# Attention's small column operations (negated maxima, edge sums, the added constant) moved from VectorE to ScalarE

## Chip, core and metric

The kernel runs on one core of a Trainium2 chip. Its time is the device time of one execution in microseconds (us). The engines are TensorE (PE in the profile; PEld is its weight load), VectorE (DVE), ScalarE (ACT), GpSimd (POOL) and SyncE (SP, which issues transfers). Each runs its own list of instructions in order, and they wait for each other by semaphores.

## What is computed

Block-sparse attention over 4 batches, 8 heads, 768 tokens and 64 columns a head, and behind it a mixture of 4 experts on the 3072 tokens with 512 columns.

```python
scores = scale * np.matmul(q, k.transpose(0, 1, 3, 2))
mask = np.abs(blk_i - blk_j) <= window          # blocks of 32, window 1
mask = mask | (blk_i == 0) | (blk_j == 0) | (blk_i == n_blocks - 1) | (blk_j == n_blocks - 1)
# ... and 3 sampled key blocks for each query block
scores = np.where(mask, scores, -1000000000.0)
scores = scores - np.max(scores, axis=-1, keepdims=True)
attn = np.exp(scores)
attn = attn / (np.sum(attn, axis=-1, keepdims=True) + 1e-09)
out = np.matmul(attn, v)
# then, on x = out by token:
p = domain_probs / (domain_probs.sum(-1, keepdims=True) + 1e-09)
for e in range(E):
    h = np.maximum(x @ w1[e], 0.0)
    y += p[:, e:e + 1] * (h @ w2[e])
```

## The kernel before

The batches run one behind the other, with attention one batch ahead: batch 0's attention alone (the first 77 us), then, while the experts work on batch b, the attention of batch b+1. Behind batch 3's attention only expert work is left. The order on all five engines is the order in which the program is written, so a queue never passes a waiting instruction.

The attention of a batch is 16 units. Four are of the class `Edge`: the first and the last query block, each against all keys in two halves (m = 0 and 1). Twelve are of the class `Group`: up to four query blocks against eight gathered key blocks each, half of the heads at a time. A unit has four steps, S, T, A and X. S makes the scores on TensorE, the maxima on VectorE and the exponentials with their sums on ScalarE. T transposes the probabilities. A multiplies them by the values and divides by the sums, X transposes the result into the experts' input `xr`. In batches 1 to 3 a unit's turn writes X of the unit before last, T of the last one, some expert work, S of the new unit, and then A of the last one. So on VectorE and ScalarE the A of a unit stands right behind the S of the next.

In a Group's S VectorE makes a masked, negated maximum (L372, the tile `mx`) for each of four heads, and ScalarE takes the exponential with this maximum as its bias and leaves the sum in `sums` (L374). A Group's A adds 1e-9 to the four sums (L402), takes the reciprocal (L403) and multiplies the result `o` in PSUM by it into `xg` (L404). An Edge's S makes two maxima (L444), for m = 1 the maximum over both halves (L446), the negated and scaled maximum `nm` (L447), for m = 1 the difference `w` of the maxima (L449), the exponentials (L451) and the exponential of the difference (L454). Its A for m = 1 adds the two halves' sums, the first weighted by `w` (L481, L482), takes the reciprocal (L483), adds the two halves of the result (L486) and multiplies (L489).

Of the experts' work these lines are spoken of. L754 is the first product and L991 (batches 1 to 3) or L827 (batch 0) the second one on TensorE. Their results go to PSUM tiles `w`, `v`, `u` and `po`, and VectorE takes them from there: L801 to L813 and L773 in batch 0, L892, L896, L899, L902 and L869 in the others, L842 adds `po` to the accumulator, L1001 adds to the totals. The tile `w` has one buffer, so the next product into it waits until VectorE has read the last (L902, L813). L914 and L915 (ScalarE, GpSimd) split the hidden layer into two parts for the second product. L158 copies sampled key blocks, L643, L679 and L718 split weights, L385 and L463 copy transposed probabilities from PSUM.

Of the kernel before, what the change touches and what calls it, by code (L numbers as in the profile page):

```python
# [8 lines left out]
F32 = mybir.dt.float32  # L9
# [3 lines left out]
AF = mybir.ActivationFunctionType  # L13
ALU = mybir.AluOpType
# [3 lines left out]
P = 128  # L18
# [5 lines left out]
def attention_moe_kernel(ctx: ExitStack, tc, qb, kb, vr, sampled, sampled_t, probs, w1, w2, out):  # L24


    nc = tc.nc
# [12 lines left out]
    SCALE = 1.0 / 8.0  # L40
# [7 lines left out]
    const = ctx.enter_context(tc.tile_pool(name="const", bufs=1))  # L48
# [6 lines left out]
    at = ctx.enter_context(tc.tile_pool(name="at", bufs=2))  # L55
# [171 lines left out]

    one = const.tile([1, 1], F32, name="one")
    nc.vector.memset(one, 1.0)
    warm = const.tile([1, 1], F32, name="warm")  # L230
    nc.scalar.activation(warm, one, AF.Exp)
    zero = p1.tile([P, HS], F32, name="zero")
# [100 lines left out]
    class Group:  # L333
# [53 lines left out]
        def A(self):  # L387
            b, t, u, n = self.b, self.t, self.u, self.n
            vs = gathered[b, t][2]
            o = pool["o"].tile([P, 2 * HH, D], F32, name="o", tag=pool["tag"])  # L390
            for m in range(2 * HH):
                e = slice((2 * HH * u + m) * D, (2 * HH * u + m + 1) * D)
                for k in range(2):
                    for c in range(n // BLOCK):
                        cs = slice(c * BLOCK, (c + 1) * BLOCK)
                        nc.tensor.matmul(o[cs, m], self.pt[:, 2 * m + k, cs], vs[c][:, k, e],  # L396
                                         start=k == 0, stop=k == 1)
            if u == 0:
                xg[0] = at.tile([P, DM], F32, name="xg", bufs=pool["xg"])
            self.xg = xg[0]  # L400
            rec = at.tile([P, 2 * HH], F32, name="rec")
            nc.vector.tensor_scalar(rec[:n], self.sums[:n], 1e-9, None, op0=ALU.add)  # L402
            nc.vector.reciprocal(rec[:n], rec[:n])  # L403
            nc.vector.tensor_mul(self.xg[:n, 2 * HH * D * u:2 * HH * D * (u + 1)]  # L404
                                 .rearrange("p (h d) -> p h d", d=D), o[:n],
                                 rec[:n].unsqueeze(2).broadcast_to([n, 2 * HH, D]))
            if u:
                gathered.pop((b, t))
# [10 lines left out]
    class Edge:  # L419
# [5 lines left out]
        def S(self):  # L425
            m = self.m
            k, q, _ = keys[self.b]
            s = [pool["s"].tile([P, HS], F32, name="sw", tag="s") for _ in range(2)]
            for hp in range(HP):
                e = slice(hp * BLOCK, (hp + 1) * BLOCK)  # L430
                for h in range(2):
                    half = slice(D * h, D * (h + 1))
                    nc.tensor.matmul(s[h][e].rearrange("p (a b) -> p a b", b=BLOCK),  # L433
                                     q[half, self.i, e], k[half, m * NB // 2:(m + 1) * NB // 2, e],
                                     start=True, stop=True)
            if m == 0:
                edge["S"] = [at.tile([P, 2, 2], F32, name=f"edge{j}") for j in range(2)]
                edge["w"] = at.tile([P, 2], F32, name="ew")
            self.mx, self.sums = edge["S"]
            self.w = edge["w"]  # L440
            self.p = pool["p"].tile([P, S], F32, name="pw", tag="p")
            nm = at.tile([P, 2], F32, name="nm2")
            for h in range(2):
                nc.vector.reduce_max(self.mx[:, m, h:h + 1], s[h], axis=AX.X)  # L444
            if m == 1:
                nc.vector.tensor_max(self.mx[:, 1], self.mx[:, 0], self.mx[:, 1])  # L446
            nc.vector.tensor_scalar(nm, self.mx[:, m], -SCALE, None, op0=ALU.mult)  # L447
            if m == 1:
                nc.vector.tensor_sub(self.w, self.mx[:, 0], self.mx[:, 1])  # L449
            for h in range(2):  # L450
                nc.scalar.activation(self.p[:, h * HS:(h + 1) * HS], s[h], AF.Exp, bias=nm[:, h:h + 1],  # L451
                                     scale=SCALE, accum_out=self.sums[:, m, h:h + 1])
            if m == 1:
                nc.scalar.activation(self.w, self.w, AF.Exp, scale=SCALE)  # L454
# [10 lines left out]
        def A(self):  # L465
            vs = keys[self.b][2]
            n = KT // 2
            o = pool["o"].tile([P, 2, D], F32, name="ow", tag=pool["tag"])
            for h in range(2):
                for k in range(n):  # L470
                    for hp in range(HP):
                        cs = slice(hp * BLOCK, (hp + 1) * BLOCK)
                        e = slice((2 * hp + h) * D, (2 * hp + h + 1) * D)
                        nc.tensor.matmul(o[cs, h], self.pt[:, h * n + k, cs], vs[self.m * n + k][:, e],
                                         start=k == 0, stop=k == n - 1)
            if self.m == 0:
                edge["o"] = at.tile([P, 2, D], F32, name="eo", bufs=1)
                pool["copy"](edge["o"], o)
                return
            rec = at.tile([P, 2], F32, name="rec2")  # L480
            nc.vector.tensor_mul(rec, self.sums[:, 0], self.w)  # L481
            nc.vector.scalar_tensor_tensor(rec, rec, 1e-9, self.sums[:, 1], op0=ALU.add, op1=ALU.add)  # L482
            nc.vector.reciprocal(rec, rec)  # L483
            eo = edge["o"]
            for h in range(2):
                nc.vector.scalar_tensor_tensor(eo[:, h], eo[:, h], self.w[:, h:h + 1], o[:, h],  # L486
                                               op0=ALU.mult, op1=ALU.add)
            self.xg = at.tile([P, P], F32, name="xe", bufs=1)
            nc.vector.tensor_mul(self.xg.rearrange("p (h d) -> p h d", d=D), eo,  # L489
                                 rec.unsqueeze(2).broadcast_to([P, 2, D]))  # L490
# [482 lines left out]
    def second7(b, c, i):  # L973
# [20 lines left out]
        for g, dh in (TO_END if last else TO)[n]:  # L994
            if c == 0 and d == 0 and n in FRESH:
                tot[g, dh] = later["a"].tile([P, 2, HS], F32, name="tot", bufs=4)
            t = tot[g, dh][:, d]
            if c == 0 and n in FRESH:
                nc.scalar.copy(t, ps)
            else:  # L1000
                nc.vector.tensor_add(t, ps, t)  # L1001
            if c == NCH - 1 and (LAST_END if last else LAST)[g, dh] == n and d:
                nc.sync.dma_start(bass.AP(out.tensor, out.offset + b * S * DM + dh * (DM // 2) * S + g * HS,
                                          [[S, P], [P * S, 2], [1, HS]]), tot.pop((g, dh)))
# [333 lines left out]
```

## Time and profile before

| | |
|---|---|
| median of 3 runs | 1234.24 us (1231.65 to 1234.75) |
| the profiled execution's time | 1232.82 us |
| its span | 1231.1 us |
| granted clock of TensorE, mean | 0.993 |
| VectorE busy, 413 to 700 us (batch 2's attention within) | 200.10 of 287 us |
| ScalarE busy in the same stretch | 119.25 of 287 us |
| TensorE busy in the same stretch | 281.08 of 287 us |

A row of the profile names line, engine, operation and tiles (out<-in). In a group's row the numbers behind the bar are the busy us, the mean ns of one, and the idle us of the engine before it with what ended it. In the order of time a row gives start and duration in us, the shape and, in brackets, the idle time before it and what released it. A row of waits gives who waited for whom: us in total, times, longest. A wait is named by its last releaser.

### The profile page before, as it was taken

How to read it: one execution, taken by the hardware profiler on the slowest of the kernel's cores; microseconds unless marked ns; L12 is line 12 of the kernel's file. 1: busy time of each engine (PE TensorE's matmuls, PEld its weight loads, DVE VectorE, ACT ScalarE, POOL GpSimd, SP SyncE). 2: the span in 40 equal slices, each digit the busy share in tenths (PEclk: the TensorE clock that was granted, in tenths of full speed). 3: DMA queues.
4: the chain of work that ended last, by engine and by line, in shares of the span. 5: the costliest groups of instructions: out<-in, count | busy, mean ns of one | idle time of the engine just before them, and what ended most of it. 6: DMA issues, size and time to landing. Idle time of an engine off the chain costs nothing.

```text
span 1231.1 us, 32030 instructions
## 1 busy us (share of the span) xinstructions
PE 1189.1 (97%) x12243; PEld 1095.4 (89%) x12243; DVE 808.7 (66%) x1701; ACT 519.8 (42%) x1259; POOL 838.4 (68%) x824
## 2 busy tenths in 40 slices
PE   7899999999999899999999999999999999999997
PEld 4678888888888898989989999989999999999997
DVE  4774757565654667767666867766566676666667
ACT  3864555656552243444533244444533333222221
POOL 7837978888776575767647775766755776666662
PEclk8999999999999899999999999999999999999999
DMA  9986869899979787888969786989876688887874
GB/s 289 264 281 232 312 246 351 290 316 318 307 266 351 227 242 233 259 278 274 270 211 345 227 267 222 286 252 283 285 253 209 219 271 266 258 262 251 255 239 154
DMA packets 214564, 326.81 MB, mean 265 GB/s; under 512 B 17483, under 2 KB 117420, under 8 KB 214412
## 3 DMA queue, kind: packets, MB, share of 16 engines
q1 hardware_dynamic: 207888, 303.53, 76.2%
q0 software_dynamic: 6480, 21.24, 5.8%
q8 instruction: 97, 1.59, 0.6%
q14 instruction: 55, 0.45, 0.1%
q10 hardware_dynamic: 44, 0.00, 0.0%
HBM read 257.02 MB, written 67.68 MB: 264 GB/s over the span
## 4 chain that ended last, share of the span: by engine, by line
PE 79%; DVE 5%; DMA 1%; issue 1%; ACT 1%; SPq 0%; POOL 0%; DVEq 0%; ACTq 0%
PE w L754 19%; PE u L991 15%; PE v L754 14%; PE v L991 12%; PE po L827 8%; PE o L396 3%; PE tp L383 2%; PE s L362 2%; PE s L355 1%; DVE ha L869 1%; PE x L415 1%; DMA pb<-prt 1%; DMA v<-in_vr_dram 1%; PE sw L433 1%; DVE tot L1001 1%
## 5 line engine op out<-in xcount | busy, mean ns | idle before, releaser
L915 POOL TENSOR_TENSOR ho<-ha,ho 128x768 fp32r<-128x768 f32 x165 | 318.3, 1938 | 244.8 <-ACT ho L914 242.0
L754 PE MATMUL w<-xo,wo 128*128 128x384 f32 x1524 | 310.9, 340 | 10.9 <-DVE ha L869 3.5
L754 PEld LDWEIGHTS w<-xo,wo 128*128 128x128 f32 x1524 | 268.8, 189 | 19.5 <-DVE ha L902 3.9
L914 ACT CAST ho<-ha 128x768 fp32r<-128x768 f32 x168 | 139.2, 837 | 269.9 <-DVE ha L869 106.1
L754 PE MATMUL v<-xo,wo 128*128 128x384 f32 x1176 | 238.9, 339 | 1.5 <-DVE xr L417 1.0
L991 PE MATMUL u<-ho,w2o 128*128 128x384 f32 x1128 | 228.2, 338 | 2.3 <-issue 2.3
L754 PEld LDWEIGHTS v<-xo,wo 128*128 128x128 f32 x1176 | 207.7, 189 | 6.4 <-DVE xr L417 1.1
L991 PEld LDWEIGHTS u<-ho,w2o 128*128 128x128 f32 x1128 | 197.0, 188 | 4.6 <-issue 2.9
L991 PE MATMUL v<-ho,w2o 128*128 128x384 f32 x888 | 179.8, 339 | 3.2 <-issue 1.5
L991 PEld LDWEIGHTS v<-ho,w2o 128*128 128x128 f32 x888 | 154.7, 188 | 7.1 <-DVE ha L869 2.7
L1001 DVE TENSOR_TENSOR tot<-v,tot 128x384 f32<-128x384 f32 x184 | 97.9, 552 | 91.6 <-PE v L991 90.3
L1001 DVE TENSOR_TENSOR tot<-u,tot 128x384 f32<-128x384 f32 x180 | 98.8, 552 | 47.9 <-PE u L991 47.8
L827 PE MATMUL po<-w2o,hh 128*128 128x512 f32 x384 | 123.5, 403 | 1.9 <-DVE oacc L842 1.9
L374 ACT ACTIVATE p<-p,mx 128x256 f32<-128x256 f32 (+1 forms) x192 | 95.3, 498 | 50.8 <-DVE mx L372 50.6
L213 POOL DMA_INDIRECT v<-in_vr_dram,vidx x81 | 79.9, 986 | 24.4 <-issue 17.8
L644 POOL TENSOR_TENSOR wo<-r,wo 128x256 fp32r<-128x256 f32 x92 | 72.4, 793 | 32.3 <-ACT wo L643 28.5
L372 DVE CUSTOM_DVE_ANT_1 p<-s,mask 128x256 f32<-128x256 f32 (+1 forms) x192 | 69.8, 419 | 22.0 <-PE s L362 17.0
L869 DVE SCALAR_TENSOR_TENSOR ha<-ha,pb 128x384 f32<-128x384 f32 x84 | 82.5, 982 | 0.0
L827 PEld LDWEIGHTS po<-w2o,hh 128*128 128x128 f32 x384 | 69.0, 188 | 12.6 <-DVE oacc L842 2.7
L827 PE MATMUL po<-w2o,hl 128*128 128x512 f32 x192 | 75.8, 395 | 0.0
L396 PEld LDWEIGHTS o<-v,pt 128*32 128x32 f32 x2816 | 46.1, 110 | 18.5 <-issue 13.5
L396 PE MATMUL o<-v,pt 128*32 128x64 f32 x2816 | 54.6, 221 | 5.1 <-issue 3.1
(169 smaller groups left out, 1627.3 us busy)
## 6 DMA issues: line engine op xcount, KB each, us to landing
w2o<-kept SPq DMA_DIRECT2D x168, 512.0 KB
wo<-kept SPq DMA_DIRECT2D x318, 256.0 KB
kept<-wo SPq DMA_DIRECT2D x106, 256.0 KB
v<-in_vr_dram SPq DMA_DIRECT2D x88, 192.0 KB
kept<-w2o SPq DMA_DIRECT2D x32, 512.0 KB
r<-in_w_dram SPq DMA_DIRECT2D x16, 512.0 KB
r<-in_w_dram SPq DMA_DIRECT2D x32, 256.0 KB
kept<-t SPq DMA_DIRECT2D x32, 256.0 KB
```

The lines of the kernel that those rows point to most:

```text
L213: nc.gpsimd.indirect_dma_start(out=v[:, i, 1 - i], out_offset=None, in_=vr, element_offset=b * S * DM, in_offset=bass.IndirectOffsetOnAxis ...
L372: nc.vector.tensor_tensor_reduce(p.rearrange("p (a b) -> p a b", b=BLOCK), s[h][:n, i], mk, -SCALE, 3.0e38, ALU.add, ALU.min, mx[:n])
L374: nc.scalar.activation(p, p, AF.Exp, bias=mx[:n], scale=-1.0, accum_out=self.sums[:n, m:m + 1])
L396: nc.tensor.matmul(o[cs, m], self.pt[:, 2 * m + k, cs], vs[c][:, k, e], start=k == 0, stop=k == 1)
L644: nc.gpsimd.tensor_sub(o[:, 1], src, f32(o[:, 0]))
L754: nc.tensor.matmul(ps, w[:, wi, t], x[:, xi, t], start=fresh and m == 0, stop=m == 3 * KH - 1, skip_group_check=not fresh)
L827: nc.tensor.matmul(p, a[:, js], w[:, i], start=f == 0 and n == 0, stop=f == FT - 1 and n == 2)
L869: nc.vector.scalar_tensor_tensor(block(g, half), src, 0.0, q, op0=ALU.max, op1=ALU.mult)
L914: nc.scalar.copy(o[:, 0], src)
L915: eng.tensor_sub(o[:, 1], src, f32(o[:, 0]))
L991: nc.tensor.matmul(ps, w[:, j, wi, ds], h[:, hi, j], start=fresh and m == 0, stop=m == 5, skip_group_check=not fresh)
L1001: nc.vector.tensor_add(t, ps, t)
```

## The change

Four small operations move. In a Group's A of batches 1 to 3 (not of batch 0) the constant 1e-9 is added by ScalarE, as a function with a bias by row from a new constant tile `eps`. In an Edge's S the negated, scaled maximum is made by ScalarE, in all batches. In an Edge's A the sum of the second half plus the constant goes to a new tile `last2` on ScalarE, and for each of the two heads the first half's sum, scaled by `w`, is added to it there with scale and bias by row; VectorE's two operations of before are gone. The reciprocals and all that follows stay on VectorE. Lines of the changed kernel below are numbered 2 to 8 higher.

```diff
+    eps = const.tile([P, 1], F32, name="eps")
+    nc.vector.memset(eps, 1e-9)
 ...
             rec = at.tile([P, 2 * HH], F32, name="rec")
-            nc.vector.tensor_scalar(rec[:n], self.sums[:n], 1e-9, None, op0=ALU.add)
+            if b:
+                nc.scalar.activation(rec[:n], self.sums[:n], AF.Identity, bias=eps[:n])
+            else:
+                nc.vector.tensor_scalar(rec[:n], self.sums[:n], 1e-9, None, op0=ALU.add)
             nc.vector.reciprocal(rec[:n], rec[:n])
 ...
-            nc.vector.tensor_scalar(nm, self.mx[:, m], -SCALE, None, op0=ALU.mult)
+            nc.scalar.mul(nm, self.mx[:, m], -SCALE)
 ...
             rec = at.tile([P, 2], F32, name="rec2")
-            nc.vector.tensor_mul(rec, self.sums[:, 0], self.w)
-            nc.vector.scalar_tensor_tensor(rec, rec, 1e-9, self.sums[:, 1], op0=ALU.add, op1=ALU.add)
+            last = at.tile([P, 2], F32, name="last2")
+            nc.scalar.activation(last, self.sums[:, 1], AF.Identity, bias=eps)
+            for h in range(2):
+                nc.scalar.activation(rec[:, h:h + 1], self.sums[:, 0, h:h + 1], AF.Identity,
+                                     bias=last[:, h:h + 1], scale=self.w[:, h:h + 1])
             nc.vector.reciprocal(rec, rec)
```

TensorE's, GpSimd's and SyncE's lists stay as they are. VectorE's list at the fourth Group unit of batch 2, before:

```order
L372 ISA p,mx<-s,mask 128x256
L372 ISA mx 128x1
L402 TENSOR_SCALAR rec<-sums 128x4
L403 RECIPROCAL rec<-rec 128x4
L404 TENSOR_TENSOR xg<-o,rec 128x256
L902 TENSOR_TENSOR ha<-w,ha 128x384
```

and now, with ScalarE's list at the same place behind it (L376 is the exponential, L910 the old L902):

```order
L374 ISA p,mx<-s,mask 128x256
L374 ISA mx 128x1
L408 RECIPROCAL rec<-rec 128x4
L409 TENSOR_TENSOR xg<-o,rec 128x256
L910 TENSOR_TENSOR ha<-w,ha 128x384
```

```order
L376 ACTIVATE p,sums<-p,mx 128x256 x4
L405 ACTIVATE rec<-sums,eps 128x4
L158 ISA
L158 COPY kr_3365<-k 128x128
L898 COPY ha<-v 128x384
```

The add has left VectorE, where it stood behind the last maximum, and stands on ScalarE behind the four exponentials of the next unit and ahead of the key copies; the reciprocal waits for it.

VectorE's list at the first Edge's A in batch 1, before:

```order
L444 TENSOR_REDUCE edge_2894<-sw 128x1 x2
L447 TENSOR_SCALAR nm_2898<-edge_2894 128x2
L481 TENSOR_TENSOR rec_2929<-edge_2518,ew 128x2
L482 SCALAR_TENSOR_TENSOR rec_2929<-rec_2929,edge_2518 128x2
L483 RECIPROCAL rec_2929<-rec_2929 128x2
L486 SCALAR_TENSOR_TENSOR eo<-eo,ew,ow 128x64 x2
L489 TENSOR_TENSOR xe<-eo,rec_2929 128x128
L813 TENSOR_TENSOR z_2824<-w,z_2824 128x384
```

and ScalarE's list at this place now (L456 is the pair of exponentials, L687 and L726 the old L679 and L718, L780 the expert's activation L772):

```order
L726 CAST t_2887<-r_2350 128x512
L452 ACTIVATE nm_2904<-edge_2900 128x2
L456 ACTIVATE pw,edge_2901<-sw,nm_2904 128x384 x2
L487 ACTIVATE last_2936<-edge_2524,eps 128x2
L489 ACTIVATE rec_2935<-edge_2524,last_2936,ew 128x1 x2
L687 CAST w2o<-r_2507 128x512
L780 ACTIVATE hh_2966<-z_2830 128x384
```

The negation stands ahead of the exponentials that use it, and the three new sums behind them; VectorE's list goes from the two maxima straight to the reciprocal.

## Prediction

> **What bounds the kernel now.** I read the page first, for the engine that sets the end: row 1 and the chain that ended last. Then the waits of TensorE, to see what still holds it up.
>
> ```profile
> PE 1189.1 (97%) x12243; PEld 1095.4 (89%) x12243; DVE 808.7 (66%) x1701; ACT 519.8 (42%) x1259; POOL 838.4 (68%) x824
> PE 79%; DVE 5%; DMA 1%; issue 1%; ACT 1%; SPq 0%; POOL 0%; DVEq 0%; ACTq 0%
> ...
> PE w L754 <- DVE ha L869: 3.5, 2, 3.2
> PE w L754 <- DVE ha L902: 3.2, 2, 1.6
> ...
> PE w L754 <- DVE z L813: 1.5, 2, 1.3
> ```
>
> TensorE is busy 97% of a span of 1231.1 us, so some 42 us of idle time are all that any change of the other engines can take away or add to. VectorE (66%) and ScalarE (42%) have room on average; moving work between them is worth only what it does to the moments at which TensorE waits for them. The waits on VectorE are few and short. So the question is not how much VectorE work goes, but whether VectorE reaches the operations that free TensorE's PSUM banks earlier or later.
>
> **What the removed operations cost.** Next the groups by line (busy us, mean ns) and, for two lines, their spread (min/median/max ns).
>
> ```profile
> L402 DVE TENSOR_SCALAR rec<-sums 128x4 f32<-128x4 f32 (+1 forms) x48 | 21.5, 448 | 0.0
> L447 DVE TENSOR_SCALAR nm<-edge 128x2 f32<-128x2 f32 x16 | 7.9, 497 | 0.7
> L482 DVE SCALAR_TENSOR_TENSOR rec<-rec,edge 128x2 f32<-128x2 f32 x8 | 5.2, 644 | 0.3
> L481 DVE TENSOR_TENSOR rec<-edge,ew 128x2 f32<-128x2 f32 x8 | 3.8, 476 | 0.0
> L374 ACT ACTIVATE p<-p,mx 128x256 f32<-128x256 f32 (+1 forms) x192 | 95.3, 498 | 50.8 <-DVE mx L372 50.6
> L643 ACT CAST wo<-r 128x256 fp32r<-128x256 f32 x92 | 36.8, 402 | 45.5 <-DVE r L639 13.1 <-issue 11.8 <-DVE r L637 7.5
> L454 ACT ACTIVATE ew<-ew 128x2 f32<-128x2 f32 x8 | 1.6, 198 | 0.0
> ...
> L402 DVE TENSOR_SCALAR rec<-sums x48: 152/220/1773, 36.3 to 937.0; 128x4 f32<-128x4 f32 x40, 64x4 f32<-64x4 f32 x8
> L403 DVE RECIPROCAL rec<-rec x48: 169/178/181, 36.5 to 937.1; 128x4 f32<-128x4 f32 x40, 64x4 f32<-64x4 f32 x8
> ```
>
> An add on four columns takes 152 ns when nothing is in its way, and up to 1773 ns; the reciprocal behind it never takes more than 181 ns. The stretched ones wait for something other than their own work, and GpSimd (68% busy) is the neighbour that could hold it. From VectorE go 36 of 48 such adds (36 x 448 ns = 16.1 us), 16 negations (7.9 us) and 16 operations of the edge sums (9.0 us): 33 us, of which about 11 are work (68 x 160 ns) and 22 waiting.
>
> ScalarE gets 36 + 16 + 8 + 16 = 76 operations. No such operation is in this trace, so its price is bounded: below by L454, a function on two columns without an operand by row (198 ns); above by that plus what a bias by row adds, read from two groups of 256 columns, 498 ns with one (L374) and 402 without (L643), so 96 ns: 294 ns, and 390 with bias and scale both by row. I take 198 for the negation, 294 for the sum plus constant, 390 for the edge's scaled sum. In all 16 x 198 + 44 x 294 + 16 x 390 ns = 22 us on an engine with 700 us free. That is no cost; the place in its queue is.
>
> The Trainium skill, "ScalarE: Activation LUTs", section Rules for kernel authors, says to give add and mul to VectorE. By unblocked rows (152 against 294 ns) the trace agrees; by the means (448 against 294 ns) it does not, and taken as a rule on busy time alone it would say some 11 us more work on an idle engine: nothing in the sum.
>
> **The place in the queue.** The add of a Group reads sums that were ready long before. On VectorE it stood behind the four masked maxima (L372) of the next unit; on ScalarE it stands behind the four exponentials that consume them, and VectorE's reciprocal now waits for it. This is the fourth unit of batch 2, with both engines and TensorE:
>
> ```profile
> 544.69 0.08 DVE L372 DVE_READ_ACCUMULATOR2_ANT mx<- 128x1 f32 x1
> 544.69 0.90 DVE L402 TENSOR_SCALAR rec<-sums 128x4 f32<-128x4 f32 x1
> 545.62 0.18 DVE L403 RECIPROCAL rec<-rec 128x4 f32<-128x4 f32 x1
> 546.24 0.55 DVE L902 TENSOR_TENSOR ha<-w,ha 128x384 f32<-128x384 f32 x1
> ...
> 545.33 0.49 ACT L374 ACTIVATE p<-p,mx 128x256 f32<-128x256 f32 x1
> 545.73 0.19 ACT L374 ACTIVATION_READ_ACCUMULATOR p<-p,mx 128x1 f32 x1
> 545.83 0.28 ACT L158 COPY kr<-k 128x128 f32 x1
> ...
> 546.85 1.31 PE L754 MATMUL w<-xo,wo 128*128 128x384 f32 x6 [1.61 <-DVE ha L902]
> ```
>
> VectorE is through with its maxima at 544.77, ScalarE with its exponentials at 545.92: 1.14 later, since an exponential takes 0.49 and a maximum 0.34. The new operation can start where L158 starts now (545.83) and ends 0.29 later; with some 0.1 for the signal the reciprocal starts at 546.22, where it started at 545.62. So a wait of about 1.45 takes the place of an add of 0.90, here 0.60 later; where the add was not stretched (0.16), about 1.33 later. Here L902 follows at once and TensorE already waits for it (1.61), so TensorE goes 0.60 later too. That the add is gone from VectorE buys nothing, because its own time lay inside the wait.
>
> Of the 36 units 33 stand behind exponentials. In each I took the lag at the reciprocal (from -0.34 to 1.45, mean 0.94 over the 36), subtracted VectorE's idle gaps in the order in which they follow, and compared what is left with the time between the end of each VectorE operation and the matmul that waits for it. In 25 of the 33 it is eaten by a gap or by TensorE's distance. In eight it reaches TensorE. The first and the last of them:
>
> ```profile
> 227.35 0.18 DVE L403 RECIPROCAL rec<-rec 128x4 f32<-128x4 f32 x1
> 227.98 1.40 DVE L842 SCALAR_TENSOR_TENSOR oacc<-po,pr,oacc 128x512 f32<-128x512 f32 x2
> 228.10 0.19 ACT L374 ACTIVATION_READ_ACCUMULATOR p<-p,mx 128x1 f32 x1
> 229.33 0.63 PE L827 MATMUL po<-w2o,hh 128*128 128x512 f32 x2
> ...
> 898.14 0.18 DVE L403 RECIPROCAL rec<-rec 128x4 f32<-128x4 f32 x1
> 899.86 0.56 DVE L902 TENSOR_TENSOR ha<-w,ha 128x384 f32<-128x384 f32 x1 [0.48 <-PE w L754]
> 898.98 0.18 ACT L374 ACTIVATION_READ_ACCUMULATOR p<-p,mx 128x1 f32 x1
> 900.70 1.03 PE L754 MATMUL w<-xo,wo 128*128 128x384 f32 x5
> ```
>
> First: lag 228.29 + 0.30 - 227.35 = 1.24; the first of the two L842 ends near 228.70, 0.6 before the matmul: 0.69 left. Last: lag 1.32, less the gap of 0.48, less 0.28 of distance and plus 0.06 for the signal: 0.62. The eight add 0.69 + 0.60 + 1.00 + 0.86 + 0.58 + 0.49 + 0.65 + 0.62 = 5.5 us. With the lower price (198 ns) it is 4.7, with 100 ns more 6.4. It is TensorE's time, and TensorE is the bound, so it stays in the total.
>
> **The edge units.** Here the negation goes first on ScalarE, then two exponentials, then the two dependent sums, and VectorE's reciprocal (L483) behind all of it.
>
> ```profile
> 154.91 0.17 DVE L483 RECIPROCAL rec<-rec 128x2 f32<-128x2 f32 x1
> 156.17 0.55 DVE L813 TENSOR_TENSOR z<-w,z 128x384 f32<-128x384 f32 x1
> 153.40 0.61 ACT L718 CAST t<-r 128x512 fp32r<-128x512 f32 x1
> 155.34 0.20 ACT L451 ACTIVATION_READ_ACCUMULATOR pw<-sw,nm 128x1 f32 x1
> 156.77 1.31 PE L754 MATMUL w<-xo,wo 128*128 128x384 f32 x6 [1.33 <-DVE z L813]
> ...
> 469.37 0.17 DVE L483 RECIPROCAL rec<-rec 128x2 f32<-128x2 f32 x1
> 471.52 0.27 PE L495 MATMUL xt<-ident,xe 128*128 128x128 f32 x1
> ```
>
> At 154 ScalarE is free at 154.01, and the negation there ends about when VectorE's did, so the exponentials end at 155.5 as before. Then 0.29 and twice 0.39, overlapping by 0.09 but with a signal between the first two, give 156.35 for the reciprocal instead of 154.91: 1.4 later, L813 follows without a gap, TensorE waits 1.4 longer. At 469 the reciprocal is 1.9 later, but the transpose waits with 1.25 in hand: 0.65. The other four of batches 1 to 3 are no later at the reciprocal than now (their sums are the stretched ones behind the means of 476 and 644 ns), or are caught by a gap. Edge sum 2.1. The negations by themselves change no path: the same length, one signal to another. The mean of 497 ns holds some 0.3 of stretching each; where TensorE waits at the end of such a chain that is spared, perhaps twice: I take -0.5.
>
> **Start.** Batch 0 has two edge sums (its Groups stay on VectorE). The first falls where both engines wait for GpSimd's queue anyway, the second makes the reciprocal 1.9 later at 33 us:
>
> ```profile
> 27.10 1.51 PE L474 MATMUL ow<-vn,ptw 128*32 128x64 f32 x48 [5.10 <-ACT ptw L463]
> 49.78 1.10 PE L352 MATMUL s<-kr,q 64*32 64x256 f32 x32 [1.43 <-DMA q<-in_qb_dram]
> ```
>
> The wait of 5.10 hides the first. The second meets a wait for a transfer of 1.43 at 49.78, so between 0 and 1.9; I take 0.5, nearer to the transfer. The constant's memset lies before the first load lands: nothing.
>
> **Sum.** 5.5 + 2.1 + 0.5 - 0.5 = 7.6 us on the profiled execution's 1232.8: 1240.4. The median of the runs shown (1234.24) is 1.4 above that execution; I leave the forecast at 1240.4. A measurement of this kernel can tell about 0.3%, 3.7 us.
>
> **Rivals.** (a) The wait is absorbed: TensorE's lost time is made up where it waits for transfers, and what VectorE no longer loses at GpSimd shortens other units. For it: 25 of 33 lags already vanish in my own count. Against: TensorE idles only 42 us, and most of that follows TensorE's own progress. 1234, chance 0.22.
>
> (b) Faster: the blocked time decides. VectorE loses 22 us to stretched small operations, and and TensorE's two waits for L902 (3.2) and two for L813 (1.5) stand behind such chains; if they go whole, 1232.8 - 4.7 = 1228. It decides if ScalarE delivers the sum before VectorE has finished its maxima, that is if exponentials end less than about 0.1 after the maxima instead of 1.14. At 544 and 898 they don't. Chance 0.12. The Trainium skill, "SBUF — State Buffer", section SBUF: two separate sides, says that VectorE and GpSimd lock one port pair against each other and that ScalarE never waits on anyone; by that rule this rival's gain is real, and the stretched rows agree, but the rule says nothing of the queue.
>
> (c) Much slower: lags also reach TensorE through ScalarE's and GpSimd's later work. All 33 passed on whole would be 34 us, with the edges 1270; a third of it gives 1251. Against: ScalarE's idle share. Chance 0.11.
>
> My forecast has 0.55, own range 1236 to 1246. Of it 0.07 lies under 1237.9. So faster 0.12, same 0.29, slower 0.59. The range 1229.5 to 1249 leaves out part of (b) and (c), below 2 in 10.
>
> **What would show it.** Right: the reciprocals of batches 1 to 3 wait for ScalarE, about 1.4 us each, 33 times; waits of TensorE for L902, L842 and L813 grow by 5 to 8 us in sum; no small operation on ScalarE above 0.4 us. Wrong: reciprocals that start within 0.2 of the last maximum, the new operations standing ahead of the exponentials in time, or waits of TensorE that shrink at the places shown.

## The result and the profile after

The changed kernel takes 1250.91 us (median, 1250.19 to 1251.81), the kernel before beside it 1233.5 us: a ratio of 1.0135, 95% interval 1.0113 to 1.0157. That is slower by 17.4 us, where 7.6 were forecast. A second measurement (after_again below) gave 1.0117, 1.0086 to 1.0148. The profiled execution of after takes 1250.19 us with a span of 1248.5; before had 1232.82 and 1231.1.

First the rows of the page that answer to those shown of before, busy time by engine and the chain that ended last:

```profile
PE 1198.9 (96%) x12243; PEld 1102.1 (88%) x12243; DVE 788.3 (63%) x1634; ACT 536.0 (43%) x1335; POOL 838.2 (67%) x824
PE 73%; DVE 6%; ACT 3%; issue 2%; DMA 2%; POOL 2%; SPq 0%; DVEq 0%; ACTq 0%; POOLq 0%
```

VectorE's busy time fell by 20 us and ScalarE's rose by 16. The operations that left VectorE had taken 34 us; the other 13 or so came back as longer durations of VectorE operations that stayed (`hl` from `z`, L781, 4.3 us more in sum, `ew` 3.4, `xe` 1.9). Two things grew on TensorE. Its idle time, span less busy time, went from 42.0 to 49.6 us: +7.6. That this is the forecast's sum to the tenth is luck: in the first 100 us it fell by 0.9 (forecast +0.5), and behind them it grew by 8.5 (forecast 7.1). And its busy time went from 1189.1 to 1198.9 us, +9.8, for the same 12243 instructions. The forecast has no term for that.

The waits of TensorE (us in total, times, longest) in after; L762, L821 and L910 are the old L754, L813 and L902, L503 the transposition of an edge's result (old L495):

```profile
PE w L762 <- DVE ha L910: 5.3, 5, 2.1
PE w L762 <- DVE z L821: 4.5, 3, 3.6
...
PE xt L503 <- DVE xe L497: 4.1, 4, 2.5
```

They were 3.2, 1.5 and 1.3 before. Together with those for `oacc` (1.9 before, 2.7 now) the waits that the prediction had said would grow by 5 to 8 us grew by 5.9. The groups by line (busy us, mean ns of one, idle time ahead and its releaser) show the new operations and the two reciprocals:

```profile
L405 ACT ACTIVATE rec<-sums,eps 128x4 f32<-128x4 f32 (+1 forms) x36 | 10.2, 283 | 0.0
L408 DVE RECIPROCAL rec<-rec 128x4 f32<-128x4 f32 (+1 forms) x48 | 8.5, 177 | 49.1 <-ACT rec L405 43.2 <-ACT p L376 4.1 <-issue 1.4
L489 ACT ACTIVATE rec<-edge,last,ew 128x1 f32<-128x1 f32 x16 | 5.3, 379 | 0.3
L452 ACT ACTIVATE nm<-edge 128x2 f32<-128x2 f32 x16 | 3.3, 204 | 43.1 <-DVE edge L449 23.5 <-DVE edge L451 14.1 <-issue 5.5
L487 ACT ACTIVATE last<-edge,eps 128x2 f32<-128x2 f32 x8 | 2.3, 286 | 0.0
L491 DVE RECIPROCAL rec<-rec 128x2 f32<-128x2 f32 x8 | 1.3, 166 | 19.2 <-ACT rec L489 17.1 <-ACT last L487 2.1
```

The prices were right within 15 ns (forecast 198, 294, 390; measured 204, 283 to 286, 379). VectorE's Group reciprocals now wait 43.2 us for ScalarE, in 30 waits of 1.44 in the mean (forecast: 33 of about 1.4).

The fourth Group unit of batch 2 in the order of time, VectorE, ScalarE and TensorE:

```profile
555.00 0.08 DVE L374 DVE_READ_ACCUMULATOR2_ANT mx<- 128x1 f32 x1
556.04 0.19 ACT L376 ACTIVATION_READ_ACCUMULATOR p<-p,mx 128x1 f32 x1
556.13 0.28 ACT L405 ACTIVATE rec<-sums,eps 128x4 f32<-128x4 f32 x1
556.44 0.18 DVE L408 RECIPROCAL rec<-rec 128x4 f32<-128x4 f32 x1 [1.36 <-ACT rec L405]
557.07 0.55 DVE L910 TENSOR_TENSOR ha<-w,ha 128x384 f32<-128x384 f32 x1
557.67 2.02 PE L762 MATMUL w<-xo,wo 128*128 128x384 f32 x6 [2.06 <-DVE ha L910]
```

The wait of the reciprocal is 1.36 (forecast 1.45), TensorE's stall goes from 1.61 to 2.06. Look at the last row's duration: six products take 2.02 us, where before they took 1.31. That is the time which no wait shows. The first edge of batch 1 has it more clearly:

```profile
159.85 0.29 ACT L487 ACTIVATE last<-edge,eps 128x2 f32<-128x2 f32 x1
160.18 0.66 ACT L489 ACTIVATE rec<-edge,last,ew 128x1 f32<-128x1 f32 x2
160.87 0.17 DVE L491 RECIPROCAL rec<-rec 128x2 f32<-128x2 f32 x1 [2.42 <-ACT rec L489]
161.43 1.26 POOL L688 TENSOR_TENSOR w2o<-r,w2o 128x512 fp32r<-128x512 f32 x1 [0.82 <-ACT w2o L687]
161.44 1.39 DVE L497 TENSOR_TENSOR xe<-eo,rec 128x128 f32<-128x128 f32 x1
162.75 0.55 DVE L821 TENSOR_TENSOR z<-w,z 128x384 f32<-128x384 f32 x1
163.36 2.29 PE L762 MATMUL w<-xo,wo 128*128 128x384 f32 x6 [3.62 <-DVE z L821]
```

TensorE stands still for 3.62 us (before 1.33), and its six products then take 2.29 us instead of 1.31. The granted clock says why. In rows by stretch (length; busy us and instructions of PE, PEld, DVE, ACT, POOL; granted TensorE clock; DMA share; GB/s), after:

```profile
157.00:162.00 5.00, 2.74 (x14) 2.08 (x12) 2.55 (x7) 3.68 (x11) 4.18 (x5) 1.00 1.03 396
162.00:170.00 8.00, 6.64 (x24) 6.20 (x25) 2.42 (x4) 3.57 (x9) 3.45 (x4) 0.57 0.85 272
553.00:558.00 5.00, 2.94 (x38) 2.52 (x27) 3.53 (x15) 2.45 (x10) 4.56 (x6) 1.00 1.04 279
558.00:562.00 4.00, 4.00 (x16) 4.00 (x15) 1.95 (x5) 0.00 (x0) 0.73 (x1) 0.57 0.95 267
```

and the same two places in before:

```profile
155.00:157.00 2.00, 0.67 (x3) 0.23 (x3) 1.68 (x5) 1.29 (x4) 1.98 (x2) 1.00 1.05 402
157.00:164.00 7.00, 7.00 (x39) 6.37 (x39) 1.67 (x3) 4.67 (x12) 5.15 (x6) 1.00 0.91 285
543.00:547.00 4.00, 2.39 (x13) 2.07 (x14) 3.86 (x14) 2.27 (x9) 3.85 (x5) 1.00 1.04 304
547.00:551.00 4.00, 4.00 (x27) 3.97 (x28) 2.31 (x5) 0.73 (x2) 1.11 (x2) 1.00 0.97 275
```

Behind the lengthened stalls the granted clock falls to 0.57 over the next 8 and 4 us; in before it stays at 1.00 and 27 products fit where after has 16.

Over the span the clock is 0.987 against 0.993: 1248.5 x 0.013 = 16.2 us lost against 1231.1 x 0.007 = 8.6, which makes 7.6 of the 9.8. But not all of it stands behind these stalls. Some 5 us of the 7.6 lie in the first 100 us, where the clock is 0.91 in after and 0.97 in before, and where kernels whose batch 0 is that of before have 0.93 to 0.97 (no_add, pad32, pad96). What the low clock behind the two stalls costs is taken from product to product further down.

### The profile page after: what moved, and what is told of

It reads as the page before. It is cut to its first block, busy times and chain, and to the rows that moved or that the text cites. A ratio compares the mean times of both kernels' runs of the same rounds, so it can differ in the third digit from the quotient of the medians.

```text
span 1248.5 us, 32005 instructions
## 1 busy us (share of the span) xinstructions
PE 1198.9 (96%) x12243; PEld 1102.1 (88%) x12243; DVE 788.3 (63%) x1634; ACT 536.0 (43%) x1335; POOL 838.2 (67%) x824
## 4 chain that ended last, share of the span: by engine, by line
PE 73%; DVE 6%; ACT 3%; issue 2%; DMA 2%; POOL 2%; SPq 0%; DVEq 0%; ACTq 0%; POOLq 0%
PE w L762 18%; PE u L999 15%; PE v L762 13%; PE v L999 11%; PE po L835 7%; PE tp L385 2%; PE o L398 2%; ACT p L376 2%; PE s L364 1%; PE s L357 1%; DVE ha L877 1%; DVE tot L1009 1%; DVE hl L781 1%; PE sw L438 1%; DMA v<-in_vr_dram 1%
## 5 line engine op out<-in xcount | busy, mean ns | idle before, releaser
L762 PE MATMUL w<-xo,wo 128*128 128x384 f32 x1524 | 311.6, 340 | 16.8 <-DVE ha L910 5.3
L762 PEld LDWEIGHTS w<-xo,wo 128*128 128x128 f32 x1524 | 268.9, 189 | 27.1 <-DVE ha L910 6.9
L762 PE MATMUL v<-xo,wo 128*128 128x384 f32 x1176 | 240.1, 340 | 1.4 <-DVE xr L422 1.0
L762 PEld LDWEIGHTS v<-xo,wo 128*128 128x128 f32 x1176 | 209.1, 190 | 6.4 <-DVE xr L422 1.1
L376 ACT ACTIVATE p<-p,mx 128x256 f32<-128x256 f32 (+1 forms) x192 | 95.3, 498 | 53.7 <-DVE mx L374 53.5
L877 DVE SCALAR_TENSOR_TENSOR ha<-ha,pb 128x384 f32<-128x384 f32 x84 | 84.0, 1000 | 0.0
L835 PEld LDWEIGHTS po<-w2o,hh 128*128 128x128 f32 x384 | 69.0, 189 | 13.4 <-DVE oacc L850 4.0
```

Of the source, the lines that this page charges most:

```text
L376: nc.scalar.activation(p, p, AF.Exp, bias=mx[:n], scale=-1.0, accum_out=self.sums[:n, m:m + 1])
L762: nc.tensor.matmul(ps, w[:, wi, t], x[:, xi, t], start=fresh and m == 0, stop=m == 3 * KH - 1, skip_group_check=not fresh)
L835: nc.tensor.matmul(p, a[:, js], w[:, i], start=f == 0 and n == 0, stop=f == FT - 1 and n == 2)
L877: nc.vector.scalar_tensor_tensor(block(g, half), src, 0.0, q, op0=ALU.max, op1=ALU.mult)
```

## The experiments

Ratios are to the kernel before on the same chip, with the 95% interval. "Idle" is TensorE's, span less busy time, in the profiled execution (before 42.0, after 49.6).

### Each part alone

group_only keeps only the first of these edits, edge_only only the others:

```diff
+            if b: nc.scalar.activation(rec[:n], self.sums[:n], AF.Identity, bias=eps[:n])
 ...
+            nc.scalar.mul(nm, self.mx[:, m], -SCALE)
+            nc.scalar.activation(last, self.sums[:, 1], AF.Identity, bias=eps)  # and the two scaled sums
```

> Only the Group addition of batches 1 to 3 on ScalarE; the edges as before. Theory 1 (the added waits of VectorE reach TensorE at a few units, and the longest of them also cost TensorE its full clock for a while): the Group places of the trace of after add to about 4.4 us of stalls, and a low clock follows the stall near 557 us, some 1.5 us: about 1239 (1237 to 1241). Theory 2 (the lags go on through ScalarE and GpSimd, the clock follows by itself): the larger part of the 17 us lies here, since 30 of the 33 reciprocals are Groups: 1245 or more. Theory 3 (the edges are all of it): 1233 to 1235.

> Only the edges' negations and sums on ScalarE; the Group addition as before. Theory 1: the stall near 157 us (2.3 us longer), the low clock behind it (about 2.5 us), 0.8 us near 471 us and about 3 us in the first 80 us, less 0.5 to 1.5 us for negations: about 1242 (1239 to 1245), with a granted clock near one half for some 7 us from 162 us on. Theory 2: 1236 or less. Theory 3: about 1250.

group_only: 1244.72 us, ratio 1.0084 (1.0065 to 1.0102), idle 48.8. edge_only: 1240.38 us, 1.0053 (1.0036 to 1.007), idle 46.2. Theory 1 had the shares wrong: the Group part cost 11.0 us, not 6, the edges 6.6, not 8. A part of the 11.0 is no wait at all, as pad32 below shows. Theory 2 comes close for the Groups (1245 or more) and misses the edges (1236 or less). That the edges are all of it (theory 3) is out.

neg_only moves only the negations, all 16:

> The kernel before, with only the eight negated edge maxima moved to ScalarE. The forecast gave -0.5 us for them, with the stretched 497 ns against 200 ns and one signal moved: 1233. If the signal or ScalarE's queue costs as for the sums: 1236 or more.

1.0003 (0.9986 to 1.002): nothing that can be told, neither the -0.5 nor +2.

no_add takes the Group addition of batches 1 to 3 out and puts nothing in its place:

```diff
+            if b: nc.vector.reciprocal(rec[:n], self.sums[:n])
```

> The Group addition of batches 1 to 3 is left out (the constant is not added there) and nothing takes its place; the edges as before. It prices what freeing VectorE of the stretched addition could bring at best. Theory 1: the addition's stretch lay in a wait for GpSimd that the reciprocal or the product behind it then meets, so 1231 to 1234. Rival (b) of the prediction, its time was on the path: 1228 or less.

1230.86 us, 0.9977 (0.9962 to 0.9992), idle 38.6. Freeing VectorE of the stretched addition is worth some 3 us: a gain smaller than rival (b)'s 4.7, but there.

### The same operations at another place in the queue

early keeps every moved operation on ScalarE and only writes each sum right behind its own unit's exponentials, so that it is done a unit ahead of the reciprocal that reads it:

```diff
 # Group.S, at its end
+            if b:
+                self.rec = at.tile([P, 2 * HH], F32, name="rec", bufs=3)
+                nc.scalar.activation(self.rec[:n], self.sums[:n], AF.Identity, bias=eps[:n])
 # Edge.S, at its end for m == 1: last and the two scaled sums; Edge.A and Group.A: rec = self.rec
```

> All of the operations stay on ScalarE, but each sum is issued right behind its own unit's exponentials and not behind those of the next unit. Theories 1 and 2 (place in ScalarE's queue decides): the reciprocals no longer wait, the stretched additions stay gone: 1229 to 1236. Rival (the operations themselves are too many or too slow for ScalarE, wherever they stand): about 1250.

1226.74 us, 0.9933 (0.9911 to 0.9955); a second time 1227.83 us, 0.9943 (0.9925 to 0.9961). The same 76 operations on the same engine are slower than before by 1.3% in one place of the queue and faster by 0.6% in another. The unit of above in early's trace (L411 is the reciprocal, L380 the addition, which belongs to the next unit now, L914 the old L902):

```profile
539.10 0.08 DVE L374 DVE_READ_ACCUMULATOR2_ANT mx<- 128x1 f32 x1
539.10 0.17 DVE L411 RECIPROCAL rec<-rec 128x4 f32<-128x4 f32 x1
...
540.29 0.30 ACT L380 ACTIVATE rec<-sums,eps 128x4 f32<-128x4 f32 x1
540.32 1.31 PE L766 MATMUL w<-xo,wo 128*128 128x384 f32 x6 [0.71 <-DVE ha L914]
```

The reciprocal starts with the last maximum, the addition of 0.90 us (before) is off VectorE's path, and TensorE's stall shrinks from 1.61 to 0.71. So the mechanism of rival (b), gain from unblocking VectorE, is real; it needs exactly the condition that the prediction named, the sum delivered before the maxima are through.

### Is it the start?

batch0_kept is after, with batch 0's two edges (negation and sums) left on VectorE.

> The changed kernel, but the two edge units of batch 0 keep negation and sums on VectorE. If batch 0's edges cost what the profile of after shows in its first 40 us (the wait for xe of 2.55 us and low clocks): 1247 to 1248. If the forecast's 0.5 us for them was right, and the rest of the start's lag is a difference between executions: 1250 to 1251.

1247.39 us, 1.0101 (1.0071 to 1.0132), against 1.0135: 3.4 thousandths, 4.2 us, but the intervals overlap, so this is not told from noise. The trace of after shows the place, ScalarE and VectorE first:

```profile
36.05 0.29 ACT L487 ACTIVATE last<-edge,eps 128x2 f32<-128x2 f32 x1
36.38 0.67 ACT L489 ACTIVATE rec<-edge,last,ew 128x1 f32<-128x1 f32 x2
37.07 0.17 DVE L491 RECIPROCAL rec<-rec 128x2 f32<-128x2 f32 x1 [2.26 <-ACT rec L489]
...
38.22 0.33 PE L503 MATMUL xt<-ident,xe 128*128 128x128 f32 x1 [2.55 <-DVE xe L497]
```

The sums stand behind a Group's four exponentials and two key copies, and TensorE waits 2.55 us at once for the transposition, and has half its clock for 3.4 us behind it. The transfer at 50 us, in which the forecast hid this, does give back its part: the wait of 1.43 is gone in after. How far behind before the same product of TensorE's list starts at 100 us tells little: 4.4 us in after, 2.2 in after_again, 5.0 in after_packed, 2.3 in batch0_kept, and 1.4 to 3.2 in pad96, no_add, pad32 and group_only, whose batch 0 is that of before. The means of the three and of the other five differ by 1.4 us, and single executions differ by more.

### Does the clock follow the standstill?

fill is after, with the 48 small products that precede the stall at 160 us computed three times (same result), so that TensorE works through part of it:

```diff
+            for _ in range(3 if self.b == 1 and self.i == 0 and self.m == 1 else 1):
```

> The changed kernel, with the 48 small products (ow) of batch 1's first edge computed three times over (the same result each time), so that TensorE works through about 1.8 us of the 3.62 us that it stood still before 163.4 us; nothing else waits for them. Theory 1 (the long standstill itself lowers TensorE's clock, and that costs 2.5 us after it): the stall shrinks to about 1.9 us, no low clock at 162 to 169 us, and the total falls although TensorE does more work: about 1248.4. Rival (the slowness after the stall comes from something else, such as weights or transfers that are late too): the low stretch stays and the total is 1251.

In the trace the stall ends at the same moment and lasts 2.28 us, and the low clock is gone:

```profile
157.00:161.00 4.00, 4.00 (x22) 3.21 (x18) 1.58 (x5) 3.33 (x11) 3.62 (x4) 1.00 1.02 389
163.30:171.00 7.70, 7.64 (x42) 6.96 (x43) 1.83 (x5) 5.37 (x13) 4.80 (x5) 1.00 0.89 288
```

Measured from product to product against before, after falls back by another 2.55 us in the 6 us behind this stall; fill by nothing. At this place, in this execution, theory 1 holds: the stall without the low clock costs its length and no more. The whole time does not confirm it: 1250.75 us, 1.0124 (1.0103 to 1.0146), within the interval of after.

fill4 fills four stalls, beside after once more:

```diff
+            for _ in range({(0, 1, 1): 2, (1, 0, 1): 3}.get((self.b, self.i, self.m), 1)):       # Edge.A
+            for m in [*range(2 * HH)] * (2 if (b, t, u) in ((2, 1, 1), (3, 0, 1)) else 1):        # Group.A
```

> The changed kernel with TensorE kept at work in four of its longest stalls: the last products of batch 0's second edge and of two Group units (near 37, 557 and 815 us in the trace of after) are computed twice, those of batch 1's first edge (near 161 us) three times, each time with the same result. No wait of VectorE or ScalarE is shorter for it. Theory 1 (behind a long standstill TensorE runs at half its clock, and that is most of what the sum of waits left out): the low clocks at 162 and 558 us are gone, one of the start may be; 2.5 + 1.5 + up to 1.5 us less than the changed kernel beside it: 1245.5 to 1247.5. Rival (the slow stretches have another cause, or come at another place in their stead): within 1.5 us of the changed kernel.

> The changed kernel again, as the measure for the one with the stalls filled: 1250 to 1252, ratio 1.012 to 1.015, mean granted clock 0.987 to 0.989.

after_again: 1248.58 us, 1.0117 (1.0086 to 1.0148), clock 0.988 to 0.993 in its six runs, somewhat better than expected. fill4: 1250.01 us, 1.0137 (1.0102 to 1.0172). A miss, and its trace says why it decides nothing. At 163 us the low clock came back although the stall was 2.27 us, as long as in fill (the last section shows why: it fell whole into one of the 3.4 us windows that are described there, and that of fill did not). At 815 us the stall shrank to 0.4 us. But at the other Group the doubled products broke off by themselves:

```profile
549.60 1.81 PE L398 MATMUL o<-v,pt 128*32 128x64 f32 x113
...
554.59 0.43 PE L398 MATMUL o<-v,pt 128*32 128x64 f32 x15 [3.18 <-issue]
```

The longer run of small products has a gap of 3.18 us of its own, in which TensorE waited for nothing that the profile shows, and that is longer than the stall of 2.06 it should have filled.

### Do the tiles' places matter?

A version that should have been the best showed a second effect on TensorE's own pace. best leaves the constant 1e-9 out everywhere: no Group addition, and the edge sums are two operations on ScalarE, issued early.

```diff
+            nc.vector.reciprocal(rec[:n], self.sums[:n])
 # Edge.S, m == 1
+                    nc.scalar.activation(rec[:, h:h + 1], self.sums[:, 0, h:h + 1], AF.Identity,
+                                         bias=self.sums[:, 1, h:h + 1], scale=self.w[:, h:h + 1])
```

> The constant 1e-9 is left out of all sums. The Group addition disappears, the edge sums become two operations on ScalarE right behind their own exponentials, the negations stay on ScalarE. If the early placement's gain of 7 us comes half from the Group additions being gone from VectorE (2.9 by the kernel without them) and half from the edges: 1225 to 1228, no worse than the early version's 1226.7. If the early version's Groups won more by their placement than by their absence: 1228 to 1231.

> The version without the constant a second time. In its first profile TensorE stood idle less than in any other (34.5 us) and still the total was that of before: TensorE's own pace was slower (177 ns from matmul to matmul of 128x384 from 1020 to 1140 us, against 173.4 before) at a granted clock of 1.00. If that belongs to the kernel (the tiles lie elsewhere once two small ones are gone): again 176 to 177 ns and a ratio of 0.998 to 1.002. If it belonged to the executions: 173.4 ns and 0.990 to 0.995.

> The early version a second time, beside the two others on one chip. If its gain belongs to the kernel: 0.991 to 0.996 of the time before, with 173.3 ns from one matmul of 128x384 to the next where TensorE is never idle (1020 to 1140 us). If it was a lucky set of executions: 0.997 or more.

> The early version with the same tiles in the same places, without the Group addition of batches 1 to 3 (the constant is left out there). If the place of tiles sets TensorE's pace, and the addition on ScalarE costs nothing when early: 173.3 ns and 0.991 to 0.996, as the early version. If leaving the addition out itself makes TensorE slower: 176 ns and 0.998 or more.

best: 0.9996 (0.9977 to 1.0016), and again 0.9995 (0.9984 to 1.0006), both with little idle time (34.5 and 36.1 us; early 35.7). early_noadd, which has the same tiles as early and no Group addition: 0.9942 (0.9924 to 0.996). So it is the kernel, not the execution, and not the missing addition. The row by stretch from 1020 to 1140 us, where TensorE is never idle and every kernel does the same expert work, first best, then best_placed:

```profile
1020.00:1140.00 120.00, 120.00 (x681) 120.00 (x680) 74.98 (x131) 30.23 (x46) 77.64 (x42) 1.00 0.81 256
```

```profile
1020.00:1140.00 120.00, 120.00 (x695) 119.97 (x694) 79.27 (x136) 30.18 (x46) 76.10 (x41) 1.00 0.80 258
```

At a granted clock of 1.00 best does 681 products and best_placed 695. best_placed is best plus two unused small tiles and a third buffer of `rec`, which puts every large tile where early has it. pad32 and pad96 are the kernel before with one or three unused small buffers of 32 bytes, at the addresses of group_only and of after; after_packed is after with its new values kept in unused parts of old tiles, at the addresses of before.

```diff
+    eps = const.tile([P, 1], F32, name="eps")       # pad32, pad96, best_placed
+            last = at.tile([P, 2], F32, name="last2")  # pad96, best_placed: never written
 # after_packed
+    one, eps = pair[:1, :1], pair[:, 1:]
+            rec, last = both[:, :2], both[:, 2:]
```

> The version without the constant, instruction for instruction but for one unused fill, with the two small tiles allocated again: the addresses of the early version. Theory 4: TensorE's pace is 173.4 ns again in place of 176.8, and the total falls by what that costs: 0.990 to 0.994 of the time before. If the pace came from the instructions that are missing: 176.8 ns and 0.998 to 1.001.

> The kernel before, with only the constant's tile added and not used: the addresses of the kernel with the Group addition alone (+32 bytes), which measured +11.0 us where its added idle time of TensorE was 6.8. Theory 4: 1.002 to 1.005, and 174.5 ns from matmul to matmul from 1020 to 1140 us, as there. Theory 1 (the slower pace came from the operations): 0.998 to 1.002 and 173.4 ns.

> The kernel before, with the changed kernel's new small tiles allocated but not used (one fill of the constant ahead of the first load): every tile lies at the addresses of the changed kernel, nothing else differs. Theory 1: the time before, 0.998 to 1.002. Theory 4: 1.002 to 1.006, with 173.9 to 174.5 ns from matmul to matmul of 128x384 in the stretch of 550 to 960 us in place of 173.5.

> The changed kernel, instruction for instruction, with the constant and the edge's second sum put into the unused part of two tiles that were there already: all large tiles lie at the addresses of the kernel before. Theory 1 (the moved operations' waits, and the clock behind them, are the 17.4 us): 1249 to 1252, ratio 1.012 to 1.015. Theory 4 (a part of the loss is the tiles' place: two or three new small tiles push every later one by 32 to 96 bytes, and TensorE then runs slower): 1243 to 1247, ratio 1.007 to 1.010.

| kernel | time, us | ratio | interval | ns from product to product, 1000 to 1150 us |
|---|---|---|---|---|
| best, best_again | 1234.87, 1234.15 | 0.9996, 0.9995 | see above | 176.8 to 177.0 |
| early_again, early_noadd | 1227.83, 1227.67 | 0.9943, 0.9942 | see above | 173.3 to 173.4 |
| best_placed | 1226.51 | 0.9937 | 0.9915 to 0.9959 | 173.4 |
| pad32 | 1237.53 | 1.0037 | 1.0022 to 1.0052 | 174.5 |
| pad96 | 1234.77 | 1.0003 | 0.9981 to 1.0025 | 173.5 |
| after_packed | 1251.16 | 1.014 | 1.0113 to 1.0166 | 173.5 |

The last column is the mean distance of the starts of successive 128x384 products of one tile in the trace; before has 173.4, group_only 174.5.

The place of tiles is worth 5.8 thousandths between best and best_placed, 3.7 in pad32, and nothing that can be told in pad96. For the change itself that settles it: its addresses alone cost nothing, and its instructions at the old addresses cost all. For group_only it matters: 8.4 - 3.7 = 4.7 thousandths, 5.8 us, are the operation's, and the rest is the place; by the two intervals the 5.8 are known to about 3 us.

## Why the prediction was wrong in size

**Right: the prices, the place in the queue, the eight Groups.** The operations cost what was said, and the reciprocal shown waits 1.36 where 1.45 was said. To see where the time went, take the start of the same product of TensorE's list in two kernels: how much further after falls behind before in a stretch is what that stretch cost. All numbers are us, places by the time in before:

| stretch | forecast | after | after_again | after_packed |
|---|---|---|---|---|
| up to 100 us | 0.5 | 4.4 | 2.2 | 5.0 |
| stall at the first edge of batch 1 (157) | 1.4 | 2.3 | 2.3 | 2.3 |
| the 13 us behind it | 0 | 2.5 | 1.4 | 1.6 |
| the eight Group places of the forecast | 5.5 | 5.1 | 5.1 | 5.2 |
| behind the two longest of these stalls (547, 803) | 0 | 1.7 | 1.6 | 1.5 |
| the edge at 471 | 0.65 | 0.8 | 0.8 | 0.8 |
| four other places (223, 293, 363, 463) | 0 | 2.2 | 2.2 | 2.2 |
| two places where TensorE waits long already (256, 403) | 0 | -1.3 | -1.4 | -1.7 |
| negations | -0.5 | not seen | not seen | not seen |
| all else | 0 | -0.3 | -0.3 | 1.5 |
| sum | 7.6 | 17.4 | 13.9 | 18.4 |

The eight Groups came as forecast, each within 0.2 us in the order of time. (The 0.6 at the last of them pad32 and pad96 show too, so that one may not be the change's.)

**The step that failed is the sum of TensorE's waits.** It priced a stall of TensorE by its length, took the work behind it as unchanged, and let all other lags be eaten. Two terms are missing, and one is too small. First, the work behind a long stall runs at half the clock for 3.4 or 6.8 us: 1.4 to 2.5 us behind the first edge and 1.5 to 1.7 behind one of the two longest Group stalls, 3.0 to 4.2 in all. That this is the clock and not the stall itself is shown by the two Group stalls, which are equally long (2.06 and 2.07 us in after, twice 2.06 in after_again). The 4 us behind each, first and second, in after and then in after_again:

```profile
557.70:561.70 4.00, 4.00 (x14) 4.00 (x15) 1.95 (x5) 0.00 (x0) 0.95 (x1) 0.57 0.97 259
818.00:822.00 4.00, 4.00 (x26) 3.97 (x27) 2.41 (x5) 0.60 (x2) 0.95 (x1) 1.00 1.05 266
...
554.30:558.30 4.00, 3.99 (x25) 3.96 (x26) 2.46 (x5) 0.54 (x2) 0.95 (x1) 1.00 0.96 265
813.10:817.10 4.00, 4.00 (x15) 4.00 (x15) 2.01 (x5) 0.00 (x0) 0.95 (x1) 0.59 0.78 234
```

Where the clock falls, 1.5 to 1.6 us more are lost; where it does not, 0.1 or less. Second, four places that the count had left out cost 2.2 us: three from the Groups (0.7, 0.3, 0.7; group_only shows them too) and one from the edges (0.5; edge_only shows it), where a VectorE operation that stayed (L877) takes 1.84 us in place of 0.62. At 256 and 403 us, where TensorE waits long already, 1.3 to 1.7 us come back.

**Mis-sized: the first edge of batch 1.** 1.4 us was said, the stall grew by 2.29. The reciprocal comes 1.65 us later, measured against the products ahead of the stall; 1.4 was said, but the terms given there (155.5, 0.29, twice 0.39, less 0.09) already make 156.48 without a signal, not 156.35. Then the product behind it (xe, L497) starts beside a GpSimd addition at 161.43 and takes 1.39 us. In before, one row of VectorE in the order of time:

```profile
155.48 0.77 DVE L489 TENSOR_TENSOR xe<-eo,rec 128x128 f32<-128x128 f32 x1
```

0.62 us more, from a shift into another neighbour's work: operations behind a moved one do not keep their length. All edges together cost 6.6 us (edge_only, with start and negations), where 2.1 + 0.5 - 0.5 = 2.1 were said.

**Mis-sized, but not settled: the start.** 0.5 us was said for batch 0's second edge. The whole time says 4.2 with wide bounds, the traces about 1.4. The start of before's profiled execution is the fastest of its kind, so the first row of the table holds chance as well.

**The rivals.** (a) is out. (b) did not happen, since the sums stood behind the next unit's exponentials; with each ahead of them, early gained 7.0 us (forecast for (b): 1228, measured 1226.74). The Trainium skill, "SBUF — State Buffer", section SBUF: two separate sides, has the gain right that way: off the port that VectorE shares with GpSimd the small operation is never stretched (L405: 283 ns in the mean, 302 at most, against 448 on VectorE). But some 13 of the 34 us came back on other VectorE operations, so freeing one operation is not freeing the engine. The rule of the Trainium skill, "ScalarE: Activation LUTs", Rules for kernel authors, to keep additions on VectorE, does not decide here: the same additions lose or win by their place. (c) named about the right time, 1251 (which takes a third of the 34 us on top of the forecast; the third alone makes 1244), by the wrong mechanism: lags beyond the forecast's places reached TensorE only at four, with 2.2 us.

**Still open.** From 100 us on the table's rows account for all but 0.3 to 1.5 of 11.7 to 13.4 us; the forecast had 7.1 there. By these executions the rest of the 15 to 17 us lies at the start, and how much of that is the change's is not shown. The parts alone make 5.8 + 6.6 = 12.4 us by the whole times; each is known to 2 or 3 us, so that they fall short of the whole is not shown either. That filling the stalls would bring the clock's part back was not shown by the whole time of fill or fill4.

## What to carry to other kernels

Before moving an operation to an idle engine, look at what stands ahead of it in that engine's queue: write it right behind the work that makes its input, not at the place where it stood before. Price a stall of TensorE by its length and by the granted clock behind it (here 1.4 to 2.5 us for each stretch of half clock), and expect the operations behind a shifted one to meet other neighbours. A variant that adds or drops a tile changes addresses: compare the pace in a stretch that the edit doesn't touch before reading its time.

## What the runs showed of the hardware

**Which standstills lower the clock.** All profiled executions from 100 us on: stalls of 3.6 us at the first edge of batch 1 were followed by a low clock (one half, for 3.4 or 6.8 us) in five of five; stalls of 2.04 to 2.13 us at the two longest Group places in 6 of 12, always at just one of the two; stalls of 1.3 to 1.7 us at these places in none of 16 (elsewhere one of 1.83 us was, in pad96). What decides is where the stall falls. The stretches of half clock start on a grid of 3.413 us: in after at 162.06, 414.65 and 558.01, which are 74 and 42 such steps apart, and so in every trace. Cut by this grid, the 19 traces have 6147 windows at full clock between 100 and 1215 us. In 34 of them TensorE stood idle for 1.83 us or more, and half clock followed each; in the other 6113 it was idle for 1.80 us at most, and half clock followed none. In after the stall of 2.06 us lies whole in the window from 554.60 to 558.01; that of 2.07 is cut at 817.42 into 1.5 and 0.5. The stall of 2.28 in fill is cut as well, into 1.0 and 1.3, and that of 2.27 in fill4 is not.

The Trainium skill, "TensorE: Matmul & The Clock Gate", Part 1: The HAM clock gate, describes a free-running window of about 3.4 us, behind which an idle TensorE gets half its clock. The grid of 3.413 us agrees with it. The rule there to leave no idle gap over about 3.4 us (section HAM oscillation — how this bites in real kernels) is too lax here, where 1.83 us idle within a window were enough.

**TensorE's pace and the place of tiles.** 32 bytes more or less ahead of the large tiles changed TensorE's steady pace at a full granted clock by up to 2% (681 against 695 products in 120 us) and the total by up to 0.6%. Shifts of 32 bytes were slow, to different degrees (best, pad32); 96 and 160 bytes (pad96, early) were not. What in the addresses does it was not tried.
